# The second visit's first-layer products behind three output tiles of the first, and its first high and low parts made at once

## The chip, the cores and the metric

One core of a Trainium2 chip. The metric is the device time of one execution in microseconds (us), the median of several runs.

## The reference

Three layers follow each other, all in float32.

```python
# 1. attention, 2 x 8 heads, 768 positions, head size 64: a window of 16 and one summary key for each block of 32
a = softmax([masked q k^T / 8, q max_block(k)^T / 8 + log 32]);  x = a @ [v, mean_block(v)]
# 2. soft mixture of experts, 8 experts with 4 slots each, x of 1536 x 512
logits = x @ phi
slots = softmax(logits, 0).T @ x;  slot_out[e] = relu(slots[e] @ w1[e]) @ w2[e]
y = softmax(logits, 1) @ slot_out                     # 1536 x 512, of rank 32
# 3. a two-layer network
h = y @ w_in;  g = max(h, 0) + log1p(exp(-abs(h)));  out = g @ w_out    # 512 -> 2048 -> 512
```

## The kernel before

The program is a list of small named tasks. Two strings, ORDER_A and ORDER_B, give the order in which they are issued, and each engine keeps the order of its own instructions. `run` reads them; no scheduler moves anything afterwards. Attention and the routing are in ORDER_A. ORDER_B starts with the expert layers and goes over into the third layer, which runs from 116 us of the span to its end and is what the change is about.

**The third layer.** As y has rank 32, the kernel computes SW = slot_out @ w_in first (tasks `swc`, `swd`, `swe`) and then h = softmax(logits, 1) @ SW. It works in 32 visits. A visit is one half R of the 1536 tokens and one block J of 128 hidden units; visits 0 and 1 are the blocks 0 and 1 of half 0, whose sum is set aside (`leave 1 t`). In visit n:

- `ha n` (`hid`, line 999): two matrix products on TensorE write h of 128 hidden units x 768 tokens to the PSUM tile `f_ps`. The pool that `f_ps` comes from has one buffer (line 702, `bufs=1`), so `ha n+1` can't start before `hx n` has read all of `f_ps`.
- `hx n` (`act`, line 1011): ScalarE applies softplus, from `f_ps` to `e`.
- `hh n` (`high`, line 1016): ScalarE copies `e` to `gh`, rounded to a shorter format.
- `hl n` (`low`, line 1021): VectorE computes `gl` = `e` - `gh` (through `less`, line 811).
- `m n t` (`gemm`, line 1029): for output tile t of 128 tokens, TensorE adds three products of 128 x 128 by 128 x 512 to `acc`: `gh` by `wh`, `gh` by `wl`, and `gl` by `wh`. The tiles t = 0, 1, 2 lie in the first half of the 768 columns, 3, 4, 5 in the second.

In visit 0 the tasks `hx`, `hh` and `hl` are cut in four: `0 0 c` is column block c of the first half (128 columns, as output tile c needs them), and `0 1` is the whole second half (384 columns).

**The weights.** w_in and w_out come in as pairs of 32-bit words, and ScalarE (`wia`, `woa`) and VectorE (`wib`, `wob`, three steps each) make float32 of them, a quarter or half a megabyte at a time, all through the first half of the third layer. `wh p` (ScalarE, `wo_hi`) and `wl p` (VectorE, `wo_lo`) then part w_out into `wh` and `wl`; both lie in one tile, `whl`. The suffix `0 0` means the first half of pair 0, which the products of visit 0 need.

**Order around the change, before.** TensorE computes SW of blocks 0 and 1 (`swc 0 0`, `swc 0 1`), then `ha 0`, `ha 1`, and then the products `m 0 1`, `m 0 5`, `m 0 4`, `m 0 2`, `m 0 3`, `m 1 3`, `m 1 2`, `m 1 1`, `ha 2`, `m 0 0`, `m 1 0`, `m 1 4`, `m 1 5`, `m 2 2`. `swd 0 1` and `swe 0 1` (VectorE) make the block of SW that `ha 1` reads.

```python
def gemm(n, *tp, hs=()):
    ...
        g = (gh, gh, gl)[p][n][:, t // 3, 128 * (t % 3):128 * (t % 3) + 128]
        mm(out=acc[(n > 1) + (n > 17), t][:, d], lhsT=g, rhs=(wh, wl, wh)[p][J][:, d], ...
```

Of the kernel before, what the change touches and what calls it, by code (L numbers as in the profile page):

```python
# [19 lines left out]
hu 2 1, w2 4 2, ht 1, hr 2, hc 1 0, dn 0 0, hc 0 1, dn 1 0, dn 0 1, w2 5 2, w2 6 2, dn 2 1, c 4, hc 1 1, wia 0 0,  # L20
wia 0 1, ht 2, dn 3 0, dn 3 1, c 3, wib 0 0 0, hu 3 0, hc 2 0, wib 0 0 1, dn 2 0, wib 0 1 0, c 5, c 6, hu 3 1, dn 4 1,
hc 2 1, dn 4 0, hr 3, ct 2, ht 3, cc 2, wib 0 1 1, wib 0 1 2, dn 5 1, hc 3 0, dn 5 0, hc 3 1, ct 1, wo 0 0 0, w2 7 1,
woa 0 0, ct 0, wo 0 0 1, dn 1 1, dn 6 1, cc 1, wob 0 0 0, dn 6 0, wib 0 0 2, dn 7 0, so 1, wob 0 0 1, yl 0, wi 0 1,
# [5 lines left out]
wo 1 0, wib 2 0, m 1 5, hl 2, leave 1 2:ACT, wi 1 1, m 2 2, m 2 1, leave 1 0:ACT, wob 1 2, leave 1 4:ACT, swa 1,
wib 2 1, woa 2, wh 1, m 2 3, wo 1 1, swb 1:ACT, ha 3, leave 1 5:DVE, m 2 0, wo 2 1, wi 2 1, wia 3, m 2 4, hx 3, hh 3,  # L30
leave 1 1:DVE, wl 1:DVE, swc 1, wib 3 0, m 2 5, swd 1:ACT, m 3 0 0, woa 3, wob 2 0, swe 1, ha 4, hx 4, hl 3, wob 3 0,
m 3 1 1, m 3 1 0, ha 5, m 3 2 1, wib 3 1, m 3 2 0, hh 4, m 4 1 0, hx 5, wib 2 2, hh 5, wi 2 0, wib 3 2, qa 1,
qb 1:ACT, m 4 0 0, qc 1, m 5 1 0, hl 5, qd 1:ACT, wob 2 1, wia 4, wob 3 1, m 4 1 1, qe 1, wob 2 2, wia 5, wh 2,
m 3 0 1, ha 6, hx 6, hl 4, wob 3 2, wib 5 0, m 5 2 1, m 5 2 0, m 4 0 1, hh 6, wib 4 0, wl 2:DVE, ha 7, m 5 0 1,
m 5 0 0, hx 7, ha 8, hh 7, m 5 1 1, m 6 0 0, m 6 1 0, wib 5 1, hl 7, m 4 2 1, wh 3, wib 5 2, m 4 2 0, wi 3 0, wib 4 1,
wia 6, hl 6, hx 8, wi 3 1, m 7 1 0, wo 2 0, woa 4, ha 9, m 6 1 1, m 7 0 1, hx 9, wib 4 2, wl 3:DVE, hh 9, m 7 1 1,
qa 2, m 9 0 0, wob 4 0, wo 3 1, m 7 2 1, qb 2:ACT, wia 7, qc 2, m 6 0 1, woa 5, qd 2:ACT, wib 6 0, m 6 2 1, hh 8,
m 7 0 0, hl 9, wob 4 1, qe 2, ha 10, wob 4 2, m 7 2 0, m 9 2 0, m 9 2 1, wob 5 0, m 9 1 1, hx 10, hh 10, wob 5 1,
wh 4, m 9 1 0, hl 8, hl 10, m 9 0 1, wl 4:DVE, m 10 0 1, m 6 2 0, wob 5 2, woa 7, m 10 0 0, ha 11, wib 7 0, hx 11,
wib 6 1, hh 11, m 8 2 0, wo 3 0, m 10 1 0, ha 12, m 10 1 1, wib 7 1, wh 5, hx 12, m 11 1 1, hl 11, m 11 0 1, m 8 1 1,  # L40
wl 5:DVE, wib 6 2, ha 13, m 8 2 1, wob 7 0, hh 12, woa 6, wib 7 2, m 11 0 0, hx 13, m 12 1 1, m 12 0 1, qa 3,
m 10 2 1, m 12 1 0, qb 3:ACT, wob 6 0, qc 3, m 11 1 0, wob 6 1, m 8 1 0, m 8 0 0, wob 6 2, m 11 2 1, m 8 0 1,
qd 3:ACT, hl 12, wh 6, qe 3, ha 14, m 10 2 0, hh 13, hx 14, m 12 0 0, wob 7 1, hl 13, ha 15, m 13 0 1, m 13 2 0,
hx 15, m 11 2 0, m 13 1 1, hh 15, wl 6:DVE, m 12 2 1, wob 7 2, ha 16, wh 7, hh 14, m 13 0 0, hl 14, m 14 0 1,
wl 7:DVE, m 12 2 0, m 14 1 1, m 15 1 0, hl 15, hx 16, ha 17, m 13 1 0, hh 16, m 13 2 1, m 15 1 1, m 14 0 0, hl 16,
m 14 1 0, m 15 2 0, m 16 0 1, hx 17, m 14 2 1, hh 17, m 16 2 1, m 14 2 0, ha 18, m 16 1 0, m 15 0 1, m 15 0 0, hx 18,
m 16 1 1, m 16 2 0, m 16 0 0, m 15 2 1, hl 17, ha 19, m 17 0, hh 18, m 17 2, m 17 5, hx 19, hh 19, m 17 1, hl 18,
hl 19, ha 20, leave 17 2:ACT, m 17 3, leave 17 0:ACT, m 17 4, leave 17 5:DVE, hx 20, ha 21, m 18 3, m 18 4,
leave 17 4:ACT, m 18 5, hx 21, hh 21, leave 17 3:DVE, hl 21, m 18 2, ha 22, m 18 0, out 17 5, leave 17 1:DVE, m 18 1,
out 17 3, m 21 0 0, m 21 2 1, hh 20, hx 22, hl 20, m 21 1 1, out 17 0, ha 23, m 20 1 1, hx 23, m 19 0 0, m 20 0 0,  # L50
out 17 2, m 21 1 0, m 19 2 0, m 20 0 1, m 20 1 0, m 21 0 1, m 19 1 0, hh 22, m 21 2 0, hl 22, m 20 2 0, m 19 0 1,
ha 24, hh 23, hx 24, m 19 2 1, hl 23, m 23 0 1, m 23 1 1, m 22 1 0, m 23 0 0, m 23 1 0, ha 25, m 22 1 1, m 22 2 0,
m 22 0 0, m 20 2 1, hh 24, m 19 1 1, hl 24, m 24 0 0, m 22 2 1, hx 25, hh 25, m 24 1 0, m 24 2 1, hl 25, ha 26,
m 22 0 1, m 24 1 1, m 24 2 0, m 25 0 1, hx 26, ha 27, hh 26, m 23 2 0, hx 27, m 24 0 1, hh 27, ha 28, m 26 0 0, hl 26,
hx 28, m 26 2 1, m 27 0 0, m 23 2 1, m 26 1 0, m 27 1 0, ha 29, m 27 0 1, hl 27, m 25 1 0, hx 29, m 25 1 1, m 27 2 1,
ha 30, m 27 1 1, hh 28, m 26 2 0, m 26 1 1, hl 28, m 28 1 1, hx 30, m 26 0 1, m 27 2 0, m 25 2 0, hh 29, m 29 1 0,
hl 29, m 25 2 1, m 25 0 0, m 28 0 0, m 29 1 1, ha 31, m 29 2 1, m 29 0 1, hh 30, m 28 2 1, out 17 1, hx 31, m 29 0 0,
hl 30, m 30 3, m 28 2 0, m 29 2 0, m 30 0, hh 31, hl 31, m 28 1 0, m 31 0, leave 31 0:DVE, m 28 0 1, out 17 4,
# [1065 lines left out]
```

## Time and profile before

| | |
|---|---|
| three runs | 276.74, 276.89, 275.98 us (median 276.74) |
| the profiled execution | 276.7 us, of which the profile's span is 274.9 us |
| granted clock of TensorE, mean | 1.000 |
| TensorE matmul (PE) | 262.8 us busy, 96% of the span |
| TensorE weight load (PEld) | 188.5 us, 69% |
| VectorE (DVE) | 161.0 us, 59% |
| ScalarE (ACT) | 146.6 us, 53% |

The shares are means over the whole span. They differ from stage to stage, so the rows further down come from single stretches. Times in the rows are counted from the start of the span; 1.8 us of the execution lie outside it.

### The profile page before, as it was taken

The page shows a single profiled execution, that of the slowest core. Times are in us where ns is not written, and L with a number is a line of the kernel's source. Part 1 is how long each engine was busy: PE and PEld are TensorE (multiplying, and loading weights), DVE is VectorE, ACT ScalarE, POOL GpSimd, SP SyncE. Part 2 cuts the span into 40 slices and gives each one's busy share as a digit, 9 for nine tenths or more (in the row PEclk, how much of TensorE's full clock was granted, in tenths as well). Part 3 has the DMA queues.
Part 4 walks back from the last instruction along what each step waited for, and adds up shares of the span by engine and source line. Part 5 has one row for each costly group of instructions (what it writes and reads, how often), then busy time and mean ns, then how long its engine had stood idle before and what let it go on. Part 6 is the DMA issues. An engine that isn't in the chain of part 4 may idle for free.

```text
span 274.9 us, 5543 instructions
## 1 busy us (share of the span) xinstructions
PE 262.8 (96%) x2312; PEld 188.5 (69%) x2312; DVE 161.0 (59%) x252; ACT 146.6 (53%) x226; POOL 34.4 (13%) x87
## 2 busy tenths in 40 slices
...
DMA packets 10280, 63.51 MB, mean 231 GB/s; under 512 B 1040, under 2 KB 1424, under 8 KB 6672
## 3 DMA queue, kind: packets, MB, share of 16 engines
...
q8 instruction: 18, 0.29, 0.4%
...
## 4 chain that ended last, share of the span: by engine, by line
PE 68%; DVE 11%; ACT 7%; DMA 6%; POOL 3%; issue 2%; SPq 1%; DVEq 0%; POOLq 0%; ACTq 0%
PE acc L1036 40%; PE h_ps L834 5%; DMA s<-in_moe_w 4%; PE av L373 3%; PE f_ps L1004 3%; PE tpa L357 3%; POOL s L267 3%; ACT s L149 3%; DMA s<-in_v 2%; PE so_ps L856 2%; ACT AB L352 2%; DVE wo L761 2%; ACT AB L149 2%; DVE gl L812 1%; PE tpx L395 1%
## 5 line engine op out<-in xcount | busy, mean ns | idle before, releaser
L1036 PE MATMUL acc<-whl,gh 128*128 128x512 f32 (+1 forms) x386 | 104.0, 391 | 0.0
L1036 PEld LDWEIGHTS acc<-whl,gh 128*128 128x128 f32 x386 | 71.4, 188 | 14.4 <-issue 0.6
L812 DVE TENSOR_TENSOR gl<-e,gh 128x768 fp32r<-128x768 f32 (+2 forms) x35 | 30.8, 886 | 56.3 <-PE acc L1036 36.3
L1036 PE MATMUL acc<-whl,gl 128*128 128x512 f32 (+1 forms) x193 | 57.2, 391 | 0.0
L1036 PEld LDWEIGHTS acc<-whl,gl 128*128 128x128 f32 x193 | 36.0, 188 | 7.6 <-DVE gl L812 0.5
L149 ACT ACTIVATE gh<-e 128x768 fp32r<-128x768 f32 (+2 forms) x35 | 27.3, 791 | 25.7 <-PE acc L1036 25.1
L1014 ACT ACTIVATE e<-f_ps 128x768 f32<-128x768 f32 (+2 forms) x35 | 26.1, 755 | 25.3 <-PE f_ps L1004 19.3
L1004 PE MATMUL f_ps<-cs 128*128 128x384 f32 x64 | 16.7, 342 | 1.5 <-DVE cs L812 1.4
L149 ACT ACTIVATE s<-s 64x520 f32<-64x520 f32 (+5 forms) x22 | 15.3, 702 | 4.3 <-DMA s<-in_v 2.5
L340 DVE TENSOR_REDUCE m<-sc 128x8 f32<-128x960 f32 x12 | 13.8, 1150 | 6.1 <-PE sc L335 6.1
L267 POOL COPY s<-vs 24x520 f32<-24x520 f32 x24 | 14.3, 619 | 16.3 <-ACT vs L149 15.2
L357 PE MATMUL tpa<-ident,AB 128*120 128x128 f32 x96 | 14.7, 283 | 1.1 <-ACT AB L352 0.7
L373 PE MATMUL av<-s,AB 120*64 120x65 f32 x384 | 15.4, 226 | 0.0
L373 PEld LDWEIGHTS av<-s,AB 120*64 120x64 f32 x384 | 12.8, 137 | 3.7 <-issue 3.3
L1004 PEld LDWEIGHTS f_ps<-cs 128*128 128x128 f32 x64 | 11.6, 188 | 4.9 <-ACT gh L149 1.7
L352 ACT ACTIVATE AB<-AB 128x480 f32<-128x480 f32 x24 | 14.1, 600 | 1.6 <-DVE AB L347 1.4
L834 PE MATMUL h_ps<-s,siT 128*32 128x512 f32 x128 | 14.5, 594 | 0.0
L347 DVE TENSOR_TENSOR AB<-sc,m 128x960 f32<-128x960 f32 x12 | 13.9, 1156 | 1.0
L149 ACT ACTIVATE AB<-tpa 120x512 f32<-120x512 f32 x23 | 13.3, 592 | 1.9 <-PE tpa L357 1.7
L753 ACT ACTIVATE wo<-wo_raw 128x1024 f32<-128x1024 f32 (+1 forms) x9 | 9.4, 1044 | 8.5 <-DMA wo_raw<-in_moe_w_out 5.9
L357 PEld LDWEIGHTS tpa<-ident,AB 128*120 128x120 f32 x96 | 10.0, 137 | 5.2 <-ACT AB L352 2.5
L856 PE MATMUL so_ps<-s,hT 128*32 128x512 f32 x104 | 12.4, 597 | 1.0 <-DMA s<-in_moe_w 1.0
...
## 6 DMA issues: line engine op xcount, KB each, us to landing
...
```

What stands on the lines that cost most here:

```text
L149: nc.scalar.activation(out=o, in_=i, func=ACTF.Copy)
L267: (nc.vector if eng == "DVE" else nc.gpsimd).tensor_copy(out=o, in_=i)
L347: nc.vector.tensor_tensor(out=A_t[i], in0=sc_t[i][:, :, 0:480].rearrange("p e (u j) -> p e u j", u=4), in1=m_t[i].rearrange("p (e u) -> p ...
L352: nc.scalar.activation(out=A_t[i][:, e], in_=A_t[i][:, e], func=ACTF.Exp, scale=0.125)
L357: nc.tensor.transpose(tp[0:120, u], A_t[i][:, e, u, :], ident)
L373: mm(out=av_t[i][64 * w:64 * w + 64, e, 65 * u:65 * u + 65], lhsT=AT_t[i][0:120, e, c:c + 64], rhs=v_t[g][0:120, 1 - w, 2 * n + t, 2 * a + ...
L812: (nc.vector if eng == "DVE" else nc.gpsimd).tensor_tensor(out=o, in0=i, in1=h.bitcast(F32), op=ALU.subtract)
L834: mm(out=h_ps[E][32 * j:32 * j + 32], lhsT=siT[:, kk], rhs=units(2 * E + j // 2, n, kk % 2, j % 2), start=(kk == 0), stop=(kk == 3), skip_ ...
L856: mm(out=so_ps[32 * m:32 * m + 32, 0], lhsT=hT[e // 4][:, e % 4, h, m], rhs=w2_t[e, h, m], start=(e == 0 and h == 0), stop=(e == 7 and h = ...
L1004: mm(out=f[n][:, h, 0:384], lhsT=cs_t["SW"][:, J], rhs=cs_t["cS"][:, s0:s0 + 384], **one)
L1014: nc.scalar.activation(out=part(e_[n], hs), in_=part(f[n], hs), func=ACTF.Softplus)
L1036: mm(out=acc[(n > 1) + (n > 17), t][:, d], lhsT=g, rhs=(wh, wl, wh)[p][J][:, d], start=(n in OPEN and p == 0), stop=(n in SHUT and p == 2) ...
```

## The change

It is a new order of the same 567 tasks, and nothing else. Three things differ in it.

- `ha 1` stands behind `m 0 1`, `m 0 5` and `m 0 4` and no longer ahead of them.
- `hh 0 0 1` stands behind the first two `hx` of visit 0 and no longer behind all four; `hl 0 0 1` stands directly behind `swe 0 1`, ahead of `wib 1 0`.
- `wh 0 0` and `wl 0 0` stand some ten tasks earlier, around `ya` (the last additions of the expert layers) and ahead of `ye 1`, the copy that makes the second half of `soT`, the slot outputs that SW is computed from.

The rest of ORDER_B is wrapped at other places with the same words, and the line numbers behind it are smaller by one.

```diff
-so 0, yl 1, wob 0 0 2, ya 0, ya 1, cc 0, yt 0, yt 1, ye 0:ACT, woa 0 1, fp, swc 0 0 0, ye 1:DVE, wob 0 1 0, swc 0 0 1,
-wh 0 0, swc 0 1 0, wob 0 1 1, swd 0 0:ACT, wia 1, swe 0 0, swc 0 1 1, wob 0 1 2, ha 0, hx 0 0 2, hx 0 0 1, hx 0 1,
-swd 0 1:DVE, wl 0 0:DVE, hx 0 0 0, hh 0 0 1, swe 0 1, hh 0 1, hh 0 0 2, wo 0 1, wib 1 0, hl 0 0 1, ha 1, wi 1 0,
...
+yl 1, wob 0 0 2, wh 0 0, ya 0, ya 1, wl 0 0:DVE, cc 0, yt 0, yt 1, ye 0:ACT, woa 0 1, fp, swc 0 0 0, ye 1:DVE, wob 0 1
+0, swc 0 0 1, swc 0 1 0, wob 0 1 1, swd 0 0:ACT, wia 1, swe 0 0, swc 0 1 1, wob 0 1 2, ha 0, hx 0 0 2, hx 0 0 1, hh 0
+0 1, hx 0 1, swd 0 1:DVE, hx 0 0 0, swe 0 1, hl 0 0 1, hh 0 1, hh 0 0 2, wo 0 1, wib 1 0, wi 1 0, m 0 1, hl 0 1, hl 0
...
```

On TensorE, from the two `ha` on, before (`f_ps_1610` and `f_ps_1629` are `ha 0` and `ha 1`; `gh_1620` and `gl_1627` are parts of visit 0, `gh_1653` and `gl_1661` of visit 1; each `acc` number is one output tile):

```order
L1004 MATMUL f_ps_1610<-cs_1330 128x384 x2
L1004 MATMUL f_ps_1629<-cs_1330 128x384 x2
L1036 MATMUL acc_1634<-whl_1598,gh_1620 128x512 x2
L1036 MATMUL acc_1634<-whl_1598,gl_1627 128x512
L1036 MATMUL acc_1642<-whl_1598,gh_1620 128x512 x2
L1036 MATMUL acc_1642<-whl_1598,gl_1627 128x512
...
L1036 MATMUL acc_1666<-whl_1598,gh_1620 128x512 x2
L1036 MATMUL acc_1666<-whl_1598,gl_1627 128x512
L1036 MATMUL acc_1666<-whl_1598,gh_1653 128x512 x2
L1036 MATMUL acc_1666<-whl_1598,gl_1661 128x512
```

The same place in the changed program (`f_ps_1611` and `f_ps_1647` are `ha 0` and `ha 1`; `gh_1617` and `gl_1623` belong to visit 0, `gh_1653` and `gl_1661` to visit 1):

```order
L1003 MATMUL f_ps_1611<-cs_1330 128x384 x2
L1035 MATMUL acc_1631<-whl_1572,gh_1617 128x512 x2
L1035 MATMUL acc_1631<-whl_1572,gl_1623 128x512
...
L1035 MATMUL acc_1643<-whl_1572,gh_1617 128x512 x2
L1035 MATMUL acc_1643<-whl_1572,gl_1623 128x512
L1003 MATMUL f_ps_1647<-cs_1330 128x384 x2
L1035 MATMUL acc_1656<-whl_1572,gh_1617 128x512 x2
L1035 MATMUL acc_1656<-whl_1572,gl_1623 128x512
L1035 MATMUL acc_1666<-whl_1572,gh_1617 128x512 x2
L1035 MATMUL acc_1666<-whl_1572,gl_1623 128x512
L1035 MATMUL acc_1666<-whl_1572,gh_1653 128x512 x2
L1035 MATMUL acc_1666<-whl_1572,gl_1661 128x512
```

Between `ha 1` and the first product of visit 1 there were five output tiles of visit 0 and now there are two.

On VectorE, from the end of the expert layers to `hl 1`, before (`so` is `ya`, `soT` is `ye 1`, `cs` is `swe 0 0`, `swd 0 1` and `swe 0 1`, `whl` is `wl 0 0`):

```order
L872 TENSOR_TENSOR so<-so_ps,so 128x256 x2
L267 COPY soT<-sT_ps 128x256
L759 TENSOR_SCALAR wo<-wo 128x512
L761 SCALAR_TENSOR_TENSOR wo<-wo_raw,wo 128x512
L812 TENSOR_TENSOR cs<-sw_ps,cs 64x128
L764 SCALAR_TENSOR_TENSOR wo<-wo_raw,wo 128x512
L267 CAST cs<-sw_ps 128x128
L812 TENSOR_TENSOR whl<-wo,whl 128x512
L812 TENSOR_TENSOR cs<-sw_ps,cs 64x128
L759 TENSOR_SCALAR wf<-wf 128x4x256
L812 TENSOR_TENSOR gl<-e,gh 128x128
```

The same place in the changed program:

```order
L871 TENSOR_TENSOR so<-so_ps,so 128x256 x2
L811 TENSOR_TENSOR whl<-wo,whl 128x512
L266 COPY soT<-sT_ps 128x256
L758 TENSOR_SCALAR wo<-wo 128x512
L760 SCALAR_TENSOR_TENSOR wo<-wo_raw,wo 128x512
L811 TENSOR_TENSOR cs<-sw_ps,cs 64x128
L763 SCALAR_TENSOR_TENSOR wo<-wo_raw,wo 128x512
L266 CAST cs<-sw_ps 128x128
L811 TENSOR_TENSOR cs<-sw_ps,cs 64x128
L811 TENSOR_TENSOR gl<-e,gh 128x128
L758 TENSOR_SCALAR wf<-wf 128x4x256
```

`wl 0 0` went ahead of the copy `ye 1`, and the first `gl` ahead of the weight step `wib 1 0`.

On ScalarE the first `gh` instruction of visit 0 stands behind two of its four `e` instructions and no longer behind all four, and `wh 0 0` went ahead of the last copy out of `ct_ps` (`cc 0`); the rest of its queue is as it was. The queues of SyncE and GpSimd are unchanged.

## Rows read from the trace of the kernel before

**Rows 1.** Busy time of each engine by stretch; mean granted clock, DMA.

```profile
core 0: us, PE busy (x) PEld busy (x) DVE busy (x) ACT busy (x) POOL busy (x), PEclk, DMA share, GB/s
117.00:124.00 7.00, 5.56 (x30) 4.40 (x29) 6.82 (x13) 5.83 (x14) 0.00 (x0) 1.00 1.02 409
124.00:146.00 22.00, 21.97 (x143) 16.51 (x142) 21.81 (x27) 17.42 (x24) 0.00 (x0) 1.00 0.72 285
146.00:270.00 124.00, 123.91 (x617) 101.95 (x616) 62.67 (x68) 57.60 (x71) 0.00 (x0) 1.00 0.12 48
```

**Rows 2.** Chain that ended last, in order of time: start, us, what.

```profile
119.09 0.61 DVE whl L812
...
123.35 0.87 DVE gl L812
...
146.03 0.02 ACT whl L149
...
147.84 0.62 PE f_ps L1004 x2
```

**Rows 3.** TensorE in order of time: start, us, instruction, count, [idle before <-releaser].

```profile
120.17 0.59 PE L1004 MATMUL f_ps<-cs 128*128 128x384 f32 x2 [1.44 <-DVE cs L812]
120.59 0.63 PE L1036 MATMUL acc<-whl,gh 128*128 128x512 f32 x2
...
121.33 0.62 PE L1036 MATMUL acc<-whl,gh 128*128 128x512 f32 x2
...
122.71 0.62 PE L1036 MATMUL acc<-whl,gh 128*128 128x512 f32 x2
...
123.39 0.62 PE L1036 MATMUL acc<-whl,gh 128*128 128x512 f32 x2
...
124.53 0.39 PE L1036 MATMUL acc<-whl,gl 128*128 128x512 f32 x1
...
126.11 0.51 PE L1004 MATMUL f_ps<-cs 128*128 128x384 f32 x2
126.46 0.62 PE L1036 MATMUL acc<-whl,gh 128*128 128x512 f32 x2
```

**Rows 4.** ScalarE in order of time.

```profile
115.60 0.38 ACT L149 ACTIVATE soT<-sT_ps 128x256 f32<-128x256 f32 x1 [1.70 <-PE sT_ps L877]
...
118.76 0.45 ACT L1014 ACTIVATE e<-f_ps 128x128 f32<-128x128 f32 x2 [0.17 <-PE f_ps L1004]
119.62 0.74 ACT L149 ACTIVATE gh<-e 128x128 fp32r<-128x128 f32 x2
...
126.66 0.81 ACT L1014 ACTIVATE e<-f_ps 128x768 f32<-128x768 f32 x1 [0.85 <-PE f_ps L1004]
127.50 0.85 ACT L149 ACTIVATE gh<-e 128x768 fp32r<-128x768 f32 x1
```

**Rows 5.** ScalarE by shape, 118.7 to 121: form, count, busy us, mean ns.

```profile
L149 ACT ACTIVATE gh<-e 128x128 fp32r<-128x128 f32 x2 | 0.7, 330 | 0.0
L149 ACT ACTIVATE gh<-e 128x384 fp32r<-128x384 f32 x1 | 0.5, 543 | 0.0
L1014 ACT ACTIVATE e<-f_ps 128x384 f32<-128x384 f32 x1 | 0.5, 498 | 0.0
```

**Rows 6.** VectorE in order of time.

```profile
114.38 0.79 DVE L872 TENSOR_TENSOR so<-so_ps,so 128x256 f32<-128x256 f32 x2 [0.20 <-PE so_ps L868]
116.05 0.42 DVE L267 COPY soT<-sT_ps 128x256 f32<-128x256 f32 x1 [0.89 <-PE sT_ps L877]
...
119.01 0.68 DVE L812 TENSOR_TENSOR whl<-wo,whl 128x512 fp32r<-128x512 f32 x1
119.72 0.29 DVE L812 TENSOR_TENSOR cs<-sw_ps,cs 64x128 fp32r<-64x128 f32 x1
...
123.27 0.95 DVE L812 TENSOR_TENSOR gl<-e,gh 128x768 fp32r<-128x768 f32 x1
```

**Rows 7.** VectorE by shape, 118.7 to 124.3.

```profile
L812 DVE TENSOR_TENSOR gl<-e,gh 128x384 fp32r<-128x384 f32 x1 | 0.6, 551 | 0.0
```

More of the change, by code (lines that the diff above doesn't have):

```diff
@@ L19 @@
 hu 2 0, wi 0 0 1, c 0, hu 0 0, c 1, hu 0 1, hu 1 0, hr 0, wi 0 0 0, w2 7 0, hu 1 1, ht 0, c 2, hc 0 0, hr 1, w2 3 2,
[L20 to L23, printed above, removed]
@@ L24 @@
-so 0, yl 1, wob 0 0 2, ya 0, ya 1, cc 0, yt 0, yt 1, ye 0:ACT, woa 0 1, fp, swc 0 0 0, ye 1:DVE, wob 0 1 0, swc 0 0 1,
-wh 0 0, swc 0 1 0, wob 0 1 1, swd 0 0:ACT, wia 1, swe 0 0, swc 0 1 1, wob 0 1 2, ha 0, hx 0 0 2, hx 0 0 1, hx 0 1,
-swd 0 1:DVE, wl 0 0:DVE, hx 0 0 0, hh 0 0 1, swe 0 1, hh 0 1, hh 0 0 2, wo 0 1, wib 1 0, hl 0 0 1, ha 1, wi 1 0,
-m 0 1, hl 0 1, hl 0 0 2, wh 0 1, wib 1 1, m 0 5, m 0 4, hx 1, wl 0 1:DVE, hh 1, wia 2, m 0 2, hh 0 0 0, hl 1, woa 1,
-wib 1 2, m 0 3, m 1 3, hl 0 0 0, m 1 2, m 1 1, leave 1 3:DVE, ha 2, wob 1 0, hx 2, m 0 0, m 1 0, hh 2, m 1 4, wob 1 1,
@@ L29 @@
[L29 to L58, printed above, removed]
+hu 2 1, w2 4 2, ht 1, hr 2, hc 1 0, dn 0 0, hc 0 1, dn 1 0, dn 0 1, w2 5 2, w2 6 2, dn 2 1, c 4, hc 1 1, wia 0 0, wia
@@ new lines @@
+0 1, ht 2, dn 3 0, dn 3 1, c 3, wib 0 0 0, hu 3 0, hc 2 0, wib 0 0 1, dn 2 0, wib 0 1 0, c 5, c 6, hu 3 1, dn 4 1, hc
+2 1, dn 4 0, hr 3, ct 2, ht 3, cc 2, wib 0 1 1, wib 0 1 2, dn 5 1, hc 3 0, dn 5 0, hc 3 1, ct 1, wo 0 0 0, w2 7 1, woa
+0 0, ct 0, wo 0 0 1, dn 1 1, dn 6 1, cc 1, wob 0 0 0, dn 6 0, wib 0 0 2, dn 7 0, so 1, wob 0 0 1, yl 0, wi 0 1, so 0,
+yl 1, wob 0 0 2, wh 0 0, ya 0, ya 1, wl 0 0:DVE, cc 0, yt 0, yt 1, ye 0:ACT, woa 0 1, fp, swc 0 0 0, ye 1:DVE, wob 0 1
+0, swc 0 0 1, swc 0 1 0, wob 0 1 1, swd 0 0:ACT, wia 1, swe 0 0, swc 0 1 1, wob 0 1 2, ha 0, hx 0 0 2, hx 0 0 1, hh 0
```

35 lines of the change are left out of this document (33 added, 2 removed).

## The prediction

> **What bounds the kernel now.** I read the busy times by stretch first. From 117 to 124 us VectorE works 6.82 of 7 us and TensorE 5.56. From 124 to 146 VectorE works 21.81 of 22 and TensorE 21.97 of 22, and from 146 to 270 TensorE works 123.91 of 124 [rows 1]. So two engines are full at once until 146 us, and behind that TensorE alone is: whatever TensorE loses at 120 us, it can't get back out of its own idle time. The chain that ended last says which of the two leads before 146. Its pieces are `wl 0 0` on VectorE at 119.09 and `gl` of visit 1 on VectorE at 123.35, it goes over to ScalarE at 146.03, and with `f_ps` at 147.84 it is on TensorE, where it stays [rows 2]. TensorE's list has one wait that strikes the eye, 1.44 us ahead of `ha 1` for the second block of SW [rows 3]. That is the hole that the change fills. The reader should see that the hole is TensorE's, while the chain at that time runs on VectorE: it stands idle for 0.89 us ahead of 116.05 [rows 6], and after that hardly at all for thirty microseconds.
>
> **What is gained first.** `wl 0 0` (0.68 us) leaves its place at 119.01, right ahead of `swe 0 1` [rows 6]. Its new place is behind `ya`, which ends at 114.38 + 0.79 = 115.17, and ahead of `ye 1` at 116.05: it takes 115.17 to 115.85 and fits into the 0.89 us of idle time. `wh 0 0` before it needs the weight step that stands ahead of `ya` on VectorE, so it can start before 114.38, and it fits into the 1.70 us in which ScalarE waits ahead of 115.60 [rows 4]. So both cost nothing there; the cover left for `wl 0 0` is 0.20 us. VectorE is 0.6 us earlier at 119.7.
>
> On ScalarE the first two `hx` end at 118.76 + 0.45 = 119.21. A copy that needs the result of the instruction ahead of it follows after 0.03 us (126.66 + 0.81 = 127.47, and 127.50) [rows 4], so `hh 0 0 1` runs from 119.24 for 0.33 [rows 5], to 119.57, where it started at 119.62 before. `m 0 1` starts some 0.1 us later, at 119.67. The 0.1 is a choice: a handoff from VectorE to TensorE takes 0.16 in one row (119.72 + 0.29 = 120.01, and `ha 1` at 120.17) [rows 3, 6], one within ScalarE 0.03. Before, `m 0 1` started at 120.59 [rows 3]. TensorE is 0.92 us ahead.
>
> **Where it goes.** `hh 0 1`, which `m 0 5` and `m 0 4` need, comes no earlier than before. Two dependent instructions of ScalarE don't overlap, two others do by 0.33 + 0.54 - 0.74 = 0.13 us [rows 4, 5]. With `hh 0 0 1` between them, `hx 0 1` runs from 119.57 - 0.13 = 119.44 to 119.94 (0.50), and `hh 0 1` from 119.97 to 120.51 (0.54) [rows 5]; before, it ended at 119.62 + 0.74 = 120.36 [rows 4]. `m 0 5` starts at 120.61 in place of 121.33 [rows 3]. Its third product needs `hl 0 1`, which takes VectorE 0.55 us [rows 7] after `hh 0 1`: 120.51 + 0.03 + 0.55 + 0.1 = 121.19. One product more (a third of the 0.68 us from one tile to the next, 122.71 to 123.39 [rows 3], so 0.23) and `m 0 4` starts at 121.42, and `ha 1` at 121.42 + 0.68 = 122.10. Before, it started at 120.17 [rows 3]: 1.93 us later.
>
> From `ha 1` on there is a chain of four that nothing shortens. `ha` takes 0.51 us without a wait, and `hx` starts 0.04 behind its end (126.11 + 0.51 = 126.62, and 126.66) [rows 3, 4]; `hx` takes 0.81, `hh` 0.03 + 0.85 [rows 4], `hl` 0.03 + 0.95 [rows 6]. So `hx 1` starts at 122.65, `hh 1` ends at 124.34 and `hl 1` at 125.32. Before, `hl 1` ended at 123.27 + 0.95 = 124.22 [rows 6]. VectorE has its queue up to `hl 1` done earlier than before, because `wl 0 0` is out of it; it now stands and waits for `hh 1`, with `wib 1 2`, the leaves and all later weight steps behind it. **VectorE comes out 1.10 us late.**
>
> TensorE has too little to do meanwhile. `ha 1` takes 0.35 us of its stream (126.11 to 126.46 [rows 3]), so `m 0 2` starts at 122.45 where it started at 122.71: of the 0.92 us of lead 0.26 are left. Two tiles more, and at 123.81 `m 1 3` is next. Its first product needs `hh 1` (124.34), its third `hl 1`: 125.32 + 0.1 = 125.42, where it stood at 124.53 [rows 3]. **TensorE comes out 0.89 us late.** In the order before, five tiles of visit 0 stood between `ha 1` and `m 1 3`; now there are two, and a chain of 0.55 + 0.81 + 0.88 + 0.98 = 3.2 us has to fit over 0.35 + 1.36 us and two products.
>
> **What stays to the end.** VectorE's 1.10 us can't be made up ahead of 146 us: it is idle for 0.19 of 22 us there [rows 1]. The chain of before goes from VectorE to ScalarE and by `f_ps` to TensorE at 146 to 148 us [rows 2], so that this wait of TensorE moves by 1.10 too. After that TensorE's idle time is 0.09 us of 124 [rows 1], and the delay goes through. The sum against the profiled execution is 276.7 + 1.1 = **277.8 us**; the median of the runs, 276.74, stands within 0.04 of that execution. Bounds: if VectorE's 0.19 is all regained, 0.91 us; with the one handoff to TensorE that is in VectorE's sum at 0.03 and not 0.1, 0.07 less; with TensorE's own 0.12 us of idle time behind 124 us regained as well, 0.7. With that handoff at 0.16, 1.2. Transfers don't come into it: SyncE's queue is the same, and the weights wait in memory for VectorE, which is the late one.
>
> **A rule against the rows.** The rows show a TensorE that idles 1.44 us [rows 3] beside a VectorE with 0.18 us of idle time in 7 [rows 1]. The Trainium skill, in "Perfetto Trace Analysis", section "Optimization Strategies", makes it the general goal to keep the matmul engine as highly utilised as possible, and to look at what blocks it when it idles. By that goal alone the change would gain; by the rows it fills TensorE's hole and opens one on the engine that leads.
>
> **The rivals.**
>
> *Faster.* TensorE keeps the lead that it has at `m 0 2`, 0.26 us, and VectorE its 0.6 us from `wl 0 0`. Then the time is 276.7 - 0.3 = 276.4, or 276.1 at best. For it speaks that the hole is real and that the lead of 0.92 us at `m 0 1` is nearly sure. It needs `hl 1` to end by 124.22 and so a chain from `ha 1` that is 1.10 us shorter than its own instructions, and nothing in the profile gives that. This is what the skill's goal of a full matmul engine amounts to here. 7 in 100.
>
> *About the same.* The loss at `m 1 3` happens, but ScalarE, idle for 4.6 of the 22 us up to 146 [rows 1], and the slack between VectorE's `gl` and their products take up a part of it, and what reaches the end is 0.2 to 0.8 us: 276.9 to 277.5. For it speaks that TensorE alone is only 0.89 us late. Against it: TensorE is full at the same time, and the chain lies on VectorE up to 146. 25 in 100.
>
> *More than forecast.* `wl 0 0` has a cover of 0.20 us. If `wh 0 0` ends later than 115.1, `ye 1` waits behind `wl 0 0`, and with it the second half of SW's products, and everything moves by what is over. At 0.5 us too late the time is 276.7 + 1.1 + 0.3 = 278.1. Against it stand the 1.70 us of free time on ScalarE. 8 in 100.
>
> TensorE's clock is granted at 1.00 in all of these stretches [rows 1], its upper level of 2.4 GHz, with the hole of 1.44 us among them; the change leaves no longer one, so I expect no fall.
>
> **How the numbers follow.** The forecast has 60 in 100. The range takes in the case of a smaller loss and the larger one, 276.9 to 278.3, and leaves out the gain and the outliers of the runs, which lie 0.9 us apart (275.98 to 276.89). What a measurement of this kernel can tell from no change is about 0.3%, or 0.83 us, so slower begins at 277.57. The forecast of 277.8 lies only 0.23 above that: with its own spread about a tenth of its 60 falls below. Slower then has 54 + 8 = 62; the same 25 + 6 = 31; faster 7.
>
> **What would show it.** In the profile of the changed kernel TensorE's 1.44 us wait ahead of `ha 1` is gone, `m 0 1` starts near 119.7 and `ha 1` near 122.1. `m 1 3` has two new waits, for `gh` of about 0.6 us and for `gl` of about 0.6 us. VectorE stands idle for more than a microsecond ahead of `hl 1`, which ends near 125.3, and `ha 2` starts near 127.0 and not at 126.11. I am wrong if `hl 1` ends by 124.3, or if it ends late and `f_ps` at 147.84 nevertheless comes at its old time.

## The result and the profile after

The changed kernel takes 278.5 us, the median of 11 runs (277.4 to 279.32), against 276.74 of the kernel before in 11 runs beside it (275.7 to 277.65). The ratio is 1.0052 [1.0035, 1.0070], so the change costs 1.44 us (0.97 to 1.94); the two medians themselves lie 1.76 us apart. Forecast were 277.8 us in a range of 276.9 to 278.3 and a chance of 0.62 for slower. The kernel is slower, as forecast. Its median lies 0.2 us above the upper end of the range; 276.74 x 1.0052, which is 278.2, lies inside it, and the 1.1 us of the forecast lie inside the interval of the cost. In a later repeat of the same kernel it is 278.18 us and a ratio of 1.0038 [1.0016, 1.0060], 1.05 us. The two intervals overlap.

The profiled execution took 279.32 us, the longest of its eleven, with a span of 277.4. Not all of its 2.6 us over the profiled execution of before (276.7) come from the change, as the first product of `yl 0` shows, a task of TensorE that stands ahead of everything that the change moves. Two rows of the kernel before, TensorE's first product of `yl 0` and its last product of the program (start, us, instruction, [idle before <-releaser]):

```profile
113.61 1.07 PE L868 MATMUL so_ps<-s,hT 128*32 128x256 f32 x16 [0.97 <-DMA s<-in_moe_w]
...
270.95 0.28 PE L1036 MATMUL acc<-whl,gl 128*128 128x256 f32 x1
```

TensorE of the changed kernel in order of time, from the same product to the same product:

```profile
114.81 1.07 PE L867 MATMUL so_ps<-s,hT 128*32 128x256 f32 x16 [0.99 <-DMA s<-in_moe_w]
...
120.86 0.74 PE L1035 MATMUL acc<-whl,gh 128*128 128x512 f32 x2 [0.94 <-ACT gh L148]
...
121.82 0.73 PE L1035 MATMUL acc<-whl,gh 128*128 128x512 f32 x2
122.42 0.50 PE L1035 MATMUL acc<-whl,gl 128*128 128x512 f32 x1
122.75 0.63 PE L1035 MATMUL acc<-whl,gh 128*128 128x512 f32 x2
...
123.45 0.51 PE L1003 MATMUL f_ps<-cs 128*128 128x384 f32 x2
...
125.73 0.73 PE L1035 MATMUL acc<-whl,gh 128*128 128x512 f32 x2 [0.39 <-ACT gh L148]
126.73 0.50 PE L1035 MATMUL acc<-whl,gl 128*128 128x512 f32 x1 [0.26 <-DVE gl L811]
127.06 0.63 PE L1035 MATMUL acc<-whl,gh 128*128 128x512 f32 x2
...
128.45 0.51 PE L1003 MATMUL f_ps<-cs 128*128 128x384 f32 x2
...
273.39 0.28 PE L1035 MATMUL acc<-whl,gl 128*128 128x256 f32 x1
```

The reader is to see two things. The program arrives at `yl 0` 1.20 us later (114.81 against 113.61), before anything that the change touches. And from there to the last product it takes 273.39 - 114.81 = 158.58 us against 270.95 - 113.61 = 157.34: **1.24 us more**. In the profile of the repeat it is 158.66, so this length comes back to 0.08 us, while the arrival at `yl 0` lies between 112.51 and 115.04 us over the profiles of all kernels here, with the same work ahead of it. Below, "the stretch" is this length, read off these two rows in each profile; it tells small effects apart that the totals blur. Of the kernel before there is one such profile, so how far its 157.34 would come back isn't known. Its ScalarE waits once for weights behind the change, at `wia 2`, and VectorE works on without a wait at that time, with `leave 1 3` in the second row:

```profile
123.41 1.16 ACT L753 ACTIVATE wf<-wi_raw 128x1024 f32<-128x1024 f32 x1 [0.75 <-DMA wi_raw<-in_moe_w_in]
...
125.59 0.69 DVE L267 COPY park<-acc 128x512 f32<-128x512 f32 x1
```

The prediction has the weights wait in memory. In the profile of the changed kernel this step waits for none; in that of the kernel before it does.

The hole of 1.44 us ahead of `ha 1` [rows 3] is gone, and what stands in its place is 0.94 us ahead of `m 0 1`, and 0.39 and 0.26 us at `m 1 3`, for `gh` and `gl` of visit 1. VectorE of the changed kernel:

```profile
116.27 0.68 DVE L811 TENSOR_TENSOR whl<-wo,whl 128x512 fp32r<-128x512 f32 x1
117.25 0.42 DVE L266 COPY soT<-sT_ps 128x256 f32<-128x256 f32 x1 [0.29 <-PE sT_ps L876]
...
125.72 0.96 DVE L811 TENSOR_TENSOR gl<-e,gh 128x768 fp32r<-128x768 f32 x1 [1.42 <-ACT gh L148]
```

Here is where the hole went: 1.42 us ahead of `hl 1`, on the engine that was idle for 0.18 us in 7 before [rows 1]. The first two rows show `wl 0 0` in its new place, and the copy `ye 1` behind it still waiting 0.29 us for TensorE, so it wasn't held up. ScalarE of the changed kernel has the links between:

```profile
120.50 0.31 ACT L148 ACTIVATE gh<-e 128x128 fp32r<-128x128 f32 x1
...
123.99 0.81 ACT L1013 ACTIVATE e<-f_ps 128x768 f32<-128x768 f32 x1 [1.51 <-PE f_ps L1003]
124.84 0.84 ACT L148 ACTIVATE gh<-e 128x768 fp32r<-128x768 f32 x1
```

`hx 1`, `hh 1` and `hl 1` follow each other with 0.04 us between them from 123.99 on (123.99 + 0.81 = 124.80, and 124.84; 124.84 + 0.84 = 125.68, and 125.72). The chain of waits of the changed kernel says the same in one view (start, us, what):

```profile
120.86 2.75 PE acc L1035 x9
...
125.72 0.96 DVE gl L811
...
148.49 0.02 ACT whl L148
...
150.30 0.62 PE f_ps L1003 x2
```

The three moved-up tiles (2.75 us) are now on the chain that ends last, ahead of `ha 1`; from `hl 1` on it runs along VectorE, goes over to ScalarE at 148.49 and is on TensorE at 150.30. Before, the chain ran along VectorE at this time, through `wl 0 0` and its neighbours [rows 2]. The busy times by stretch, with the columns of [rows 1], the last three cut 1.20 us later than there:

```profile
60.00:100.00 40.00, 38.59 (x421) 18.52 (x422) 15.80 (x52) 13.44 (x26) 1.90 (x2) 0.96 0.98 399
118.20:125.20 7.00, 6.06 (x30) 4.17 (x28) 5.66 (x11) 4.98 (x12) 0.00 (x0) 1.00 1.03 421
125.20:147.20 22.00, 21.35 (x136) 15.41 (x136) 21.32 (x25) 17.40 (x25) 0.00 (x0) 1.00 0.67 266
147.20:271.20 124.00, 123.91 (x617) 102.01 (x616) 63.12 (x67) 58.73 (x73) 0.00 (x0) 1.00 0.13 50
```

In the 7 us around the change TensorE is busier by 0.50 us than before (6.06 for 5.56) and VectorE less so by 1.16 (5.66 for 6.82). Behind 147.2 us TensorE works 123.91 of 124, as before: nothing can be given back there.

### The profile page after: what moved, and what is told of

Same layout as the page of the kernel before. It is cut to its first block, busy times and chain, and to the rows that moved or that the text cites. A ratio compares the mean times of both kernels' runs of the same rounds, so it can differ in the third digit from the quotient of the medians.

```text
span 277.4 us, 5545 instructions
## 1 busy us (share of the span) xinstructions
PE 265.4 (96%) x2312; PEld 188.7 (68%) x2312; DVE 161.1 (58%) x252; ACT 147.1 (53%) x226; POOL 34.6 (12%) x87
## 4 chain that ended last, share of the span: by engine, by line
PE 70%; DVE 9%; ACT 8%; DMA 6%; POOL 3%; issue 2%; SPq 1%; DVEq 0%; ACTq 0%; POOLq 0%
PE acc L1035 41%; PE h_ps L833 6%; PE f_ps L1003 4%; DMA s<-in_moe_w 4%; PE av L372 3%; PE tpa L356 3%; POOL s L266 3%; DMA s<-in_v 3%; ACT s L148 2%; PE so_ps L855 2%; ACT AB L351 2%; ACT AB L148 1%; PE tpx L394 1%; DVE wo L760 1%; DVE wf L763 1%
## 5 line engine op out<-in xcount | busy, mean ns | idle before, releaser
L833 PE MATMUL h_ps<-s,siT 128*32 128x512 f32 x128 | 16.2, 652 | 0.0
L334 PE MATMUL sc<-s 64*64 64x120 f32 x384 | 12.2, 263 | 0.5 <-DMA s<-in_k 0.5
```

The costliest lines, as they stand in the source:

```text
L833: mm(out=h_ps[E][32 * j:32 * j + 32], lhsT=siT[:, kk], rhs=units(2 * E + j // 2, n, kk % 2, j % 2), start=(kk == 0), stop=(kk == 3), skip_ ...
```

## The experiments

One table first. "Stretch" is from the start of the first product of `yl 0` to that of the last product in the profile of the run, "against before" the difference to 157.34. The last column is by how much later than before VectorE ends `hl 2`, counted from the same first product (before: 128.66 + 0.95 - 113.61 = 16.00 us). The ratio is that of the totals, against the kernel before on the same chip. Line numbers differ by one between kernels, as ORDER_B is wrapped differently.

| kernel | median us | ratio [95%] | stretch, from and to | against before | `hl 2` late |
|---|---|---|---|---|---|
| changed | 278.5 | 1.0052 [1.0035, 1.0070] | 158.58 (114.81, 273.39) | +1.24 | +1.25 |
| after_again (changed, repeated) | 278.18 | 1.0038 [1.0016, 1.0060] | 158.66 (113.92, 272.58) | +1.32 | +1.27 |
| wl_early | 276.59 | 0.9996 [0.9978, 1.0015] | 156.89 (113.65, 270.54) | -0.45 | -0.45 |
| ha_back | 279.53 | 1.0095 [1.0067, 1.0122] | 160.25 (112.51, 272.76) | +2.91 | +2.94 |
| ha_front | 276.41 | 0.9991 [0.9964, 1.0018] | 157.13 (113.18, 270.31) | -0.21 | -0.25 |
| one_tile | 277.25 | 1.0017 [0.9994, 1.0041] | 157.06 (114.57, 271.63) | -0.28 | -0.26 |
| two_tiles | 278.08 | 1.0044 [1.0018, 1.0070] | 157.90 (115.04, 272.94) | +0.56 | +0.58 |
| fill_v | 278.15 | 1.0042 [1.0028, 1.0056] | 158.18 (114.03, 272.21) | +0.84 | +0.88 |
| fill_t | 278.18 | 1.0037 [1.0018, 1.0056] | 158.39 (113.85, 272.24) | +1.05 | +1.07 |
| fill_both | 277.24 | 1.0025 [0.9998, 1.0053] | 158.22 (113.11, 271.33) | +0.88 | +0.89 |
| fill_ha2 | 277.59 | 1.0030 [0.9998, 1.0063] | 157.80 (114.41, 272.21) | +0.46 | +0.49 |
| one_leave | 276.64 | 0.9969 [0.9948, 0.9990] | 156.82 (114.21, 271.03) | -0.52 | -0.62 |
| wl_leave | 276.52 | 0.9973 [0.9951, 0.9995] | 157.34 (113.29, 270.63) | 0.00 | -0.13 |

The theory: `ha 1` starts too late, its chain over ScalarE ends at `hl 1`, VectorE comes out late and stays so. The rivals: that the other parts of the change lose the time (`wl 0 0`, the early `hh`), that TensorE's own lateness at `m 1 3` decides and not VectorE's, or that a part of the loss is made up on the way.

### The change again: after_again

The changed kernel was run once more, with no edit, beside later experiments.

> The changed kernel once more, beside the others on one chip. Theory: from the first product of yl 0 to the last product it takes 158.58 us again, within 0.1, and the total differs from run to run by what the stages ahead of it take. Rival (the 1.23 us over before are partly chance of one execution, as a clock that fell elsewhere): a value that differs by 0.3 or more.

Its stretch is 158.66 us, where the first profile has 158.58, and its ratio 1.0038 [1.0016, 1.0060]: slower again.

### The parts apart: wl_early and ha_back

**wl_early** is the kernel before with `wh 0 0` and `wl 0 0` alone in their new places.

```
  yl 1, wob 0 0 2
+ wh 0 0
  ya 0, ya 1
+ wl 0 0:DVE
  cc 0, yt 0
...
  wob 0 1 0, swc 0 0 1
- wh 0 0
  swc 0 1 0, wob 0 1 1
...
  hx 0 1, swd 0 1:DVE
- wl 0 0:DVE
  hx 0 0 0, hh 0 0 1
```

> The kernel before, with wh 0 0 and wl 0 0 early as in the change and nothing else of it. Theory (VectorE leads up to 146 us, and the loss of the change comes from ha 1 standing further back): wl 0 0 costs nothing at its new place and takes 0.6 us out of VectorE's queue ahead of swe 0 1, so ha 1 starts 0.3 us earlier (ScalarE frees f_ps at 119.76) and hl 1 ends 0.6 us earlier: 276.1 to 276.4 us, 0.3 to 0.6 below before. Rival (the early wh 0 0 and wl 0 0 push back ye 1 and with it SW): 0.2 to 0.5 above before.

The stretch is 0.45 us shorter, within the 0.3 to 0.6 of the theory. The ratio, 0.9996 [0.9978, 1.0015], can't show so little. So this part loses nothing, and in the profile it gains.

**ha_back** is the kernel before with `ha 1` alone moved.

```
  wib 1 0, hl 0 0 1
- ha 1
  wi 1 0, m 0 1
...
  m 0 5, m 0 4
+ ha 1
  hx 1, wl 0 1:DVE
```

> The kernel before, with ha 1 behind m 0 1, m 0 5 and m 0 4 and nothing else of the change. Theory: m 0 1 waits for wl 0 0 and the late hh 0 0 1, ha 1 starts near 122.6, hl 1 ends near 125.9, VectorE is 1.6 us late and TensorE 1.4: 278.2 to 278.4 us, more than the whole change. Rival (the early hh 0 0 1 with its dependent instructions on ScalarE is what costs): within 0.3 of before.

The sign was right and the size was not: 160.25, 2.91 us more than before. The rows put the excess down to TensorE's clock. The busy times by stretch of ha_back:

```profile
118.00:120.00 2.00, 0.84 (x3) 0.40 (x3) 1.94 (x5) 1.98 (x7) 0.00 (x0) 1.00 1.02 418
120.00:121.00 1.00, 1.00 (x4) 0.81 (x5) 1.00 (x3) 0.00 (x0) 0.00 (x0) 0.79 1.01 410
121.00:122.00 1.00, 1.00 (x3) 0.79 (x3) 1.00 (x2) 0.00 (x0) 0.00 (x0) 0.50 1.09 438
122.00:123.00 1.00, 1.00 (x4) 0.82 (x3) 0.25 (x1) 0.00 (x0) 0.00 (x0) 0.50 0.99 406
123.00:124.00 1.00, 1.00 (x5) 0.81 (x4) 0.00 (x0) 0.62 (x1) 0.00 (x0) 0.51 1.03 426
```

and TensorE of ha_back in order of time:

```profile
118.90 0.74 PE L1036 MATMUL acc<-whl,gh 128*128 128x512 f32 x2 [1.28 <-ACT gh L149]
...
120.24 0.76 PE L1036 MATMUL acc<-whl,gh 128*128 128x512 f32 x2
...
121.22 1.05 PE L1036 MATMUL acc<-whl,gh 128*128 128x512 f32 x2
...
122.50 0.84 PE L1004 MATMUL f_ps<-cs 128*128 128x384 f32 x2
```

The clock is granted at 0.50, the level of 1.2 GHz, from 121 to 124 us. It fell in the microsecond before (0.79 in the mean), behind two, 118 to 120, in which TensorE worked 0.84. From one tile to the next it takes 0.98 and 1.28 us there in place of 0.68 [rows 3], which puts `ha 1` 0.90 us later, and `ha 1` itself takes 0.84 in place of 0.51: 1.23 us of the excess of 1.3 over the expected 1.6. The changed kernel has 1.00 in the whole stretch from 118.2 us on, so this is no part of its loss. It does show what the rest of the change is good for: `m 0 1` comes at 6.05 us behind `yl 0` with it (120.86 - 114.81) and at 6.39 without it (118.90 - 112.51).

### How many tiles ahead of ha 1: ha_front, one_tile, two_tiles

All three keep the rest of the change and differ only in the place of `ha 1`: ahead of `m 0 1`, behind it, and behind `m 0 5`. The edit of one_tile:

```
  wi 1 0, m 0 1
+ ha 1
  hl 0 1, hl 0 0 2
...
  m 0 5, m 0 4
- ha 1
  hx 1, wl 0 1:DVE
```

In two_tiles the added `ha 1` stands between `m 0 5` and `m 0 4`, in ha_front between `wi 1 0` and `m 0 1`.

> The changed kernel with ha 1 back ahead of all product tiles; the early hh 0 0 1, hl 0 0 1, wh 0 0 and wl 0 0 stay. Theory: ScalarE frees f_ps 0.35 us later than before (120.11 for 119.76) because hh 0 0 1 stands ahead of the last hx, so ha 1 starts when it did before though swe 0 1 is 0.6 us earlier; hl 1 ends 0.3 us earlier: the stretch is 157.05 to 157.35, the time 276.4 to 276.7. Rival (the early hh 0 0 1 is part of the loss): 157.6 or more.

> The changed kernel with ha 1 behind m 0 1 alone. Theory: ha 1 starts near 6.75 us after the first product of yl 0 and ScalarE, which is at wh 0 1 until 7.6, starts hx 1 when it did in the order with ha 1 ahead; hl 1 ends 0.2 to 0.3 us earlier than before and TensorE is earlier too: the stretch is 157.0 to 157.15, the time 276.4 to 276.5. Rival (any product tile ahead of ha 1 costs its length): 157.8.

> The changed kernel with ha 1 behind m 0 1 and m 0 5, and m 0 4 behind it. Theory: ha 1 near 7.9 us after the first product of yl 0, hl 1 ends 0.4 to 0.55 us later than before, TensorE 0.2 late: the stretch is 157.75 to 157.9, the time 277.2. Rival (the loss doesn't come from where ha 1 stands): 158.6, as in the changed kernel.

With 0, 1, 2 and 3 tiles ahead of `ha 1` the stretch is 157.13, 157.06, 157.90 and 158.58; the first three lie within what was expected. The first tile is free (the 0.07 us between the first two are within the 0.08 by which the changed kernel came back): it lies in the hole. `ha 1` then starts 6.85 us behind `yl 0` and 6.60 without it, and these 0.25 us don't reach `hx 1`, for ScalarE has `wh 0 1` ahead of it and starts `hx 1` without a wait, at 7.56 and 7.58 us, in both. Each tile more costs 0.84 and 0.68, about the time of a tile (0.68 us [rows 3]). All of the loss is in the second and third tile, and none in the early `hh` and `wl`. The totals rise with the number of tiles (276.41, 277.25, 278.08, 278.5), also over the first one, but those of the first two can't be told from the kernel before.

### Which engine brings the loss to the end: fill_v and fill_t

**fill_v** is the changed kernel with a weight step of VectorE (`wib 1 2`, 1.22 us) moved into its hole ahead of `hl 1`. VectorE is then hardly late, and TensorE's waits at `m 1 3` stay.

```
  m 0 2, hh 0 0 0
+ wib 1 2
  hl 1, woa 1
- wib 1 2
  m 0 3, m 1 3
```

> The changed kernel, with the weight step wib 1 2 of VectorE ahead of hl 1, so that VectorE works in the time in which it waits for hh 1. hl 1 ends when it did in the changed kernel, but VectorE's queue behind it is only 0.3 us late. Theory (VectorE's lateness is what reaches the end): TensorE is 0.9 us late at m 1 3 and gets back what it waited for VectorE and ScalarE further on in the kernel before, 0.4 to 0.5 us: 277.2 us, 0.4 to 0.5 above before, 0.7 below the changed kernel. Rival (TensorE's own wait at m 1 3 is what reaches the end): 277.6, 0.9 above before.

VectorE and TensorE of fill_v at that place:

```profile
123.43 1.22 DVE L764 SCALAR_TENSOR_TENSOR wf<-wi_raw,wf 128x1024 int32<-128x1024 int32 x1
124.94 0.96 DVE L812 TENSOR_TENSOR gl<-e,gh 128x768 fp32r<-128x768 f32 x1 [0.29 <-ACT gh L149]
126.16 0.29 DVE L812 TENSOR_TENSOR gl<-e,gh 128x128 fp32r<-128x128 f32 x1 [0.26 <-ACT gh L149]
...
129.95 0.96 DVE L812 TENSOR_TENSOR gl<-e,gh 128x768 fp32r<-128x768 f32 x1 [0.21 <-ACT gh L149]
```

```profile
124.96 0.73 PE L1036 MATMUL acc<-whl,gh 128*128 128x512 f32 x2 [0.39 <-ACT gh L149]
...
127.68 0.51 PE L1004 MATMUL f_ps<-cs 128*128 128x384 f32 x2
```

VectorE waits 0.29 us ahead of `hl 1` in place of 1.42, and the stretch is still 0.84 us longer than before, as the rival has it and the theory has not. VectorE's rows show how. With `wib 1 2` done ahead, VectorE's queue is late by next to nothing at `hl 1`, but it waits again at both of its next `gl`, 0.26 and 0.21 us. The first is `hl 0 0 0`, whose `hh 0 0 0` stands behind the late `hh 1` in ScalarE's queue. The second is `hl 2`, since `ha 2` starts 127.68 - 114.03 = 13.65 us behind `yl 0`, as in the changed kernel (128.45 - 114.81 = 13.64) and not as before (126.11 - 113.61 = 12.50). The chain of waits of fill_v goes this second way, from `m 1 3` behind `hl 1` over `ha 2`, `hx 2` and `hh 2` to `hl 2`:

```profile
125.95 1.88 PE acc L1036 x7
...
127.84 0.36 PE f_ps L1004 x2
...
129.07 0.86 ACT gh L149
```

At `hl 2` VectorE is 0.88 us late again. So TensorE's lateness at `m 1 3` is enough to bring the loss, and it comes back to VectorE by the chain from `ha 2`; filling VectorE's hole alone doesn't help much.

**fill_t** is the counterpart: a tile of visit 0 (`m 0 0`, with its `hh` and `hl`) moved between `m 0 3` and `m 1 3`, so that TensorE has work while `hl 1` is late.

```
  m 0 4, ha 1
+ hh 0 0 0
  hx 1, wl 0 1:DVE
...
  wia 2, m 0 2
- hh 0 0 0
+ hl 0 0 0
  hl 1, woa 1, wib 1 2, m 0 3
+ m 0 0
  m 1 3
- hl 0 0 0
  m 1 2, m 1 1
...
  wob 1 0, hx 2
- m 0 0
  m 1 0, hh 2
```

> The changed kernel, with output tile m 0 0 ahead of m 1 3 (and hh 0 0 0 and hl 0 0 0, which it needs, early), so that TensorE has a tile more to do while it waits for visit 1. TensorE is then 0.2 us late at m 1 3, VectorE 0.9 us late behind hl 1. Theory (VectorE's lateness is what reaches the end): TensorE waits for gl of visit 2 in place of that of visit 1, 277.6 us, 0.9 above before. Rival (TensorE's own wait at m 1 3 is what reaches the end): 276.9, 0.2 above before.

VectorE of fill_t still has its hole, and no wait behind it:

```profile
124.77 0.96 DVE L812 TENSOR_TENSOR gl<-e,gh 128x768 fp32r<-128x768 f32 x1 [1.23 <-ACT gh L149]
125.65 1.22 DVE L764 SCALAR_TENSOR_TENSOR wf<-wi_raw,wf 128x1024 int32<-128x1024 int32 x1
...
129.97 0.95 DVE L812 TENSOR_TENSOR gl<-e,gh 128x768 fp32r<-128x768 f32 x1
```

TensorE has a whole tile more done ahead of `m 1 3`, and the stretch is 1.05 us longer than before all the same. VectorE is 1.07 us late at `hl 2`, the 1.27 of `hl 1` (124.77 + 0.96 - 113.85 = 11.88 us behind `yl 0`, before 10.61) less the `gl` that it had done ahead. Here the theory is right, and the rival's small loss is out: VectorE's lateness goes to the end, with no new wait of VectorE to feed it. TensorE waits for `gl` of visit 2, at `m 2 2`, as the theory says:

```profile
130.98 0.50 PE L1036 MATMUL acc<-whl,gl 128*128 128x512 f32 x1 [0.43 <-DVE gl L812]
```

### Both holes filled: fill_both and fill_ha2

**fill_both** makes both edits.

> The changed kernel with both fillings: m 0 0 ahead of m 1 3 on TensorE and wib 1 2 ahead of hl 1 on VectorE. Theory as it stands now (each engine's lateness at visit 1 reaches the end by itself, and the larger of the two decides): TensorE is 0.2 us late and VectorE 0.35 (the copy leave 1 3 waits for m 1 3), so the stretch from the first product of yl 0 to the last product is 0.2 to 0.4 us above the 157.35 of before: 157.6 to 157.75, and the time about 277.1. Rival (only one of the two matters, VectorE's or TensorE's): 0.8 above, as with one filling, 158.2. Rival (the early hh 0 0 1 and wl 0 0 cost something of their own): 158 or more.

A miss: 0.88 us stay, no less than in fill_v. The number is that of both rivals. The second of them is out by ha_front and wl_early, whose stretches are shorter than before; the first doesn't fit fill_v and fill_t, where each of the two engines was enough. VectorE of fill_both:

```profile
124.03 0.96 DVE L812 TENSOR_TENSOR gl<-e,gh 128x768 fp32r<-128x768 f32 x1
125.58 0.69 DVE L267 COPY park<-acc 128x512 f32<-128x512 f32 x1 [0.59 <-PE acc L1036]
...
129.04 0.96 DVE L812 TENSOR_TENSOR gl<-e,gh 128x768 fp32r<-128x768 f32 x1 [0.30 <-ACT gh L149]
```

VectorE has no wait ahead of `hl 1` now, and gets two behind it: 0.59 us at `leave 1 3`, the copy of the late tile `m 1 3`, and 0.30 at `hl 2`, for `ha 2` stands behind `m 1 1` in TensorE's queue and is as late as ever. Only the second decides when `hl 2` starts: 129.04 - 113.11 = 15.93 us behind `yl 0`, and 129.95 - 114.03 = 15.92 in fill_v, which has no wait at the copy.

**fill_ha2** takes that up: fill_both with `ha 2` ahead of `m 1 3`.

```
  m 0 3, m 0 0
+ ha 2
  m 1 3, m 1 2, m 1 1, leave 1 3:DVE
- ha 2
  wob 1 0, hx 2
```

> As fill_both, with ha 2 ahead of m 1 3 as well. fill_both missed its number by 0.6 us; theory for that: ha 2 came 1.1 us late in it, the same chain of four ran from ha 2 to hl 2, and the loss came back at visit 2. Then with ha 2 early TensorE is 0.1 us ahead at m 1 3, VectorE 0.4 late (leave 1 3 waits for m 1 3), hl 2 no longer waits for hh 2, and the stretch from the first product of yl 0 to the last product is 157.6 to 157.8 (0.25 to 0.45 above before), the time about 277.2. Rival (VectorE's 0.4 us and the order of its queue are what keeps fill_both late, ha 2 is not): 158.1 to 158.3, as fill_both.

VectorE of fill_ha2:

```profile
126.88 0.69 DVE L267 COPY park<-acc 128x512 f32<-128x512 f32 x1 [0.59 <-PE acc L1036]
127.49 0.68 DVE L759 TENSOR_SCALAR wo<-wo 128x1024 int32<-128x1024 int32 x1
...
129.95 0.95 DVE L812 TENSOR_TENSOR gl<-e,gh 128x768 fp32r<-128x768 f32 x1
```

The wait at `hl 2` is gone, and the stretch falls from 158.22 to 157.80, 0.46 us above before, at the end of what was expected. The wait at `leave 1 3` is left. VectorE starts this copy 126.88 - 114.41 = 12.47 us behind `yl 0`, 0.49 later than before (125.59 - 113.61 = 11.98), and at `hl 2` it is still 0.49 late. So the 0.46 that stay are there at the copy already. But the copy needn't be their only cause. The weight step behind it, `wob 1 0` at 127.49, reads what `woa 1` on ScalarE makes, and that ends at 126.22 + 1.11 = 127.33, late as `hx 1` is:

```profile
126.22 1.11 ACT L753 ACTIVATE wo<-wo_raw 128x1024 f32<-128x1024 f32 x1
```

So had the copy not waited, `wob 1 0` could have begun only some 0.1 us earlier. No run takes the two apart.

### A faster version: one_leave and wl_leave

Since VectorE is full up to 146 us [rows 1] and ScalarE isn't, the copy `leave 1 3` can go to ScalarE. **one_leave** is one_tile with that, **wl_leave** is wl_early with it.

```
  m 1 2, m 1 1
- leave 1 3:DVE
+ leave 1 3:ACT
  ha 2, wob 1 0
```

> As one_tile, with the copy leave 1 3 (0.69 us) on ScalarE in place of VectorE. In one_tile TensorE was 0.37 us ahead of before at m 1 3 and VectorE 0.25. Theory (the slower of the two decides): VectorE is then 0.9 ahead behind hl 1, TensorE's 0.37 decide, and its small waits for VectorE up to 148 us shrink: the stretch is 156.6 to 156.9, the time 276.0 to 276.4. Rival (VectorE's queue has slack there): 157.07 as one_tile.

> As wl_early, with the copy leave 1 3 on ScalarE in place of VectorE. TensorE was 0.35 us ahead of before at ha 1 in wl_early and 0.46 at the end. Theory (the slower of the two decides): VectorE 1.1 us ahead, TensorE's 0.35 and its small waits decide: the stretch is 156.6 to 156.85, the time 275.9 to 276.3. Rival (VectorE's queue has slack there): 156.9 as wl_early.

one_leave is faster than the kernel before, by little: 276.64 us, ratio 0.9969 [0.9948, 0.9990], and its stretch is 156.82, as expected, though its total lies above the 276.0 to 276.4. wl_leave has a like ratio, 0.9973 [0.9951, 0.9995], but its profile doesn't show the gain: its stretch is 157.34, a miss. ScalarE of wl_leave:

```profile
123.32 1.17 ACT L753 ACTIVATE wf<-wi_raw 128x1024 f32<-128x1024 f32 x1 [0.97 <-DMA wi_raw<-in_moe_w_in]
```

and VectorE behind it:

```profile
125.74 0.69 DVE L759 TENSOR_SCALAR wo<-wo 128x1024 int32<-128x1024 int32 x1 [0.73 <-ACT wo L753]
```

In that execution the weights of a step came late; ScalarE waited 0.97 us and VectorE 0.73 behind it. In the profile of wl_early, and in that of one_leave, the same step of ScalarE has no such wait; the kernel before has one of 0.75 us, which `leave 1 3` on VectorE covered. How often it falls in the other runs isn't known, so why the median gains all the same stays open.

## Why the prediction was right, and where not

Every step can be held against the trace; times of the changed kernel with 1.20 us taken off, the later arrival at `yl 0`. The last row is the prediction's 147.84 with its 1.10 us added.

| step | before | forecast | measured |
|---|---|---|---|
| `m 0 1` starts | 120.59 | 119.67 | 119.66 |
| `m 0 5` starts | 121.33 | 120.61 | 120.62 |
| `ha 1` starts | 120.17 | 122.10 | 122.25 |
| `hl 1` ends | 124.22 | 125.32 | 125.48 |
| third product of `m 1 3` starts | 124.53 | 125.42 | 125.53 |
| `ha 2` starts | 126.11 | 127.0 | 127.25 |
| `f_ps` at 147.84 starts | 147.84 | 148.94 | 149.10 |

**The gain at first** came as worked out: 0.93 us at `m 0 1`, for 0.92. `wh 0 0` and `wl 0 0` cost nothing in their new places (0.29 us of idle time left ahead of `ye 1`, for 0.20), and wl_early shows this part alone with a shorter stretch. The rival in which the cover of `wl 0 0` breaks is out.

**The loss** has the forecast's mechanism: the dose of tiles in ha_front, one_tile, two_tiles and the changed kernel shows that it is the place of `ha 1` and nothing else of the change. Its size was too small at one term: the way from `m 0 5` to `ha 1`. The forecast took one product more, 0.23 us, behind the third product of `m 0 5`, and 0.68 for `m 0 4`. The rows of the changed kernel have 122.75 - 122.42 = 0.33 and 123.45 - 122.75 = 0.70. With 0.03 us from the products ahead of it, `ha 1` is late by 2.08 and not 1.93, VectorE by 125.48 - 124.22 = 1.26 and not 1.10, and the stretch by 1.24 and 1.32. At `m 1 3` it is the same: behind the product that waited for `gl` the next starts 127.06 - 126.73 = 0.33 later, so TensorE is late by 1.00 there and by 1.11 one product on, where the forecast had 0.89. Its two waits at `m 1 3` are 0.39 and 0.26 us in the view, for about 0.6 each in the forecast; counted from start to start they are near it. The first product starts at 125.73 and not at 123.45 + 0.35 + 1.36 = 125.16, and the third 1.00 us behind it and not two thirds of 0.68, so both are 0.55 us or a little more late.

**What stays to the end** was right: between `hl 1` and the last product nothing is made up. VectorE is 1.26 us late there, the last product 1.24, and the rival "about the same", in which ScalarE's idle time takes up a part, is out for this kernel. The way is the forecast one: `f_ps`, which the prediction named as the test, is 150.30 - 1.20 - 147.84 = 1.26 us late too. The reason holds for the changed kernel and for fill_t, where the chain runs along VectorE; in fill_t VectorE has no wait behind `hl 1` by which another engine could add to it. Over the thirteen runs of the table the lateness of VectorE at `hl 2` is the lateness of the last product to within 0.13 us, whether it is -0.62 or +2.94, but that alone doesn't say which engine leads, and one correction is needed. The forecast took the losses of the two engines for separate ones, of which VectorE's is the larger. fill_v and fill_both show that TensorE's, at `m 1 3`, comes back to VectorE by way of `ha 2` and `hl 2`, and fill_ha2 that with `ha 2` early a part stays by the leave or by `woa 1`. VectorE would have been late by `hl 2` even with its own hole filled. TensorE can also carry a delay by itself: in two_tiles the chain of waits is on TensorE from `m 1 3` (126.28) to the last product, with no piece on VectorE between, and the stretch is 0.56 us longer. No run has TensorE alone late, with VectorE on time.

**Faster** is out: the lead of TensorE at `m 0 1` was real, and it was used up at `m 1 3`. It also answers the prediction's rule against the rows: TensorE's busy time in the 7 us rose from 5.56 to 6.06, and the kernel lost. In the 22 us behind them it fell from 21.97 to 21.35, so over both stretches TensorE is no fuller than before: 27.41 us for 27.53.

**The median** of 278.5 lies above the range's end of 278.3, the repeat's 278.18 inside it. 276.7 + 1.24 to 1.32 would be 277.9 to 278.0 by the stretches; the rest of the 278.5 lies ahead of the change or in the spread of the runs, and the profiles don't tell which.
